# Fused windowed attention and token/channel mixer: scores of both halves in one row-tiled run, regroups moved to a second buffer pair, and emission order on all engines

## The chip, the cores and the metric

One NeuronCore of a Trainium2 chip. The metric is the device time of one execution in microseconds (us), median over several runs. Ratios are the mean time of one kernel's fast runs over the mean of the other's fast runs of the same rounds, so they are not quite the ratio of the medians quoted.

The time of one and the same kernel moves by up to 1% with the start of the program. Secondly, what comes after that point repeats well: wherever two kernels have the same items in a stage, the stage's length agreed within some 0.02 us. So beside the whole time I use **the stretch**: from the first weight load of tok1 of batch 1 to the last weight load of the program. It is read from the trace.

## The reference, cut to what matters

```python
# q, k, v: (8 batches, 8 heads, 576 positions, 64)
scores = scale * q @ k.T;  mask: 0 <= q_pos - k_pos < 128, with a slope per head
x = softmax(scores) @ v                       # per head, then heads side by side: (8, 576, 512)
h = relu(x.T @ w_tok1) @ w_tok2               # token mixing, 576 -> 256 -> 576
u = x + h.T
out = u + relu(u @ w_ch1) @ w_ch2             # channel mixing, 512 -> 1536 -> 512
```

## The kernel before

All matmuls and transposes run on TensorE (PE), with VectorE (DVE) and ScalarE (ACT) copying their results out of PSUM, the memory that they are written to. A "regroup" is a VectorE copy that puts a batch's q or k in the order that the transposes read. Attention goes by pairs of heads, g = 4 * batch + pair. The attention of batch b+1 is "side" work, spread between the mixer's items of batch b by weights. A pair needs four steps: transposes of q and k (`att_T`), scores with exp and mask in two halves (`att_S`), the product with the values (`att_V`). The scores are "row-tiled": each matmul uses 64 of TensorE's 128 rows, one head on each half. "Emission order" is the order in which the program names the instructions.

```python
ps_at = tile_pool(bufs=2, PSUM)     # two slots of two banks: transposes, scores, values
ps_ma = tile_pool(bufs=4, PSUM)     # four slots of one bank: the mixer

def regroup(b, h0, h1, which=(0, 1)):            # VectorE, one buffer qg, one kg
    for n in which:
        raw, t = ((qn, qg), (kn, kg))[n]
        nc.vector.tensor_copy(out=t[...], in_=raw[b % 2][...].rearrange("p h (j d) -> p j h d", j=6))

def att_T(g):
    ...                                          # 12 transposes of qg, kg into one two-bank tile
    nc.scalar.copy(out=dst(qT[g % 4]), in_=nat(0))
    nc.vector.tensor_copy(out=dst(kT[g % 4]), in_=nat(1))
    if hp == 3 and 0 < b < B - 1:
        regroup(b + 1, 0, H)                     # behind the last pair of a batch
        if b + 3 < B: dma_qk(b + 3, 0, H)

def att_S(g, half):
    sp = ps_at.tile([P, 2, 512], f32)            # a slot
    ...                                          # 4 or 6 matmuls with 64 of 128 rows, heads on
                                                 # rows 0-63 and 64-127
    for i in range(2): nc.scalar.activation(out=pe[:, i, :], in_=sp[:, i, :], func=Exp, ...)
    nc.vector.tensor_tensor(out=pb, in0=pe, in1=masks[...], op=mult)

def att_V(g):
    ...                                          # 18 matmuls into ot, then on VectorE:
    nc.vector.reciprocal(out=rt, ...);  nc.vector.tensor_tensor(out=xb[b][...], in0=ot, in1=rt)

def att_step(g):
    return [(0.6, att_T(g + 2)), (0.5, att_S(g + 1, 0)), (0.5, att_S(g + 1, 1)), (0.6, att_V(g))]

# mixer of a batch: tok1, tok2 (ht; VectorE: ub = ht + xb), trans_u (ut; VectorE: UT = ut),
# ch1 (ct; ScalarE: relu -> R), and ch2 of the batch before (o2; VectorE: obt = o2 + ub)

with tc.manual_schedule():                       # start, batch 0, attention of batch 1
    ...
with tc.manual_schedule(engines={PE}):           # the rest: PE in emission order, the other
    ...                                          # engines as a scheduler orders them
```

The softmax here doesn't subtract the row's maximum and nothing guards it: scores larger than these inputs give would overflow.

## Time and profile before

| | before |
|---|---|
| median | 334.01 us (333.99 to 334.29) |
| span of the profiled run | 332.9 us |
| the stretch (tok1 of batch 1 to the end) | 263.68 us |

The page of the kernel before: busy time by engine, and the clock in tenths over 40 slices of the span.

```profile
PE 307.6 (92%) x2816; PEld 189.1 (57%) x2816; DVE 178.9 (54%) x340; ACT 178.5 (54%) x373; POOL 60.9 (18%) x81
...
PEclk9999989999799999999999999999999999999999
```

PE is the bound. But "busy" hides what matters here, as matmuls overlap and their ends are modelled: one has to look at the distance from one start to the next. Within a stage these distances are constant (121.5 ns for 288 columns, 216 ns for 512). Whatever is above them is a loss, and losses are small here. The next lines are the timeline of PE alone: start, time, operation, count.

```profile
172.49 0.39 PE L234 MATMUL sp<-qT_93,kT_97 64*128 64x256 bf16 x4
172.81 1.64 PE L352 MATMUL ct<-UT,WC_105 128*128 128x288 bf16 x12
174.39 0.39 PE L234 MATMUL sp<-qT_93,kT_97 64*128 64x256 bf16 x6
174.71 0.54 PE L352 MATMUL ct<-UT,WC_105 128*128 128x288 bf16 x3
```

The two runs of `sp` (scores) are the two halves of one pair. The last ct ahead of the first run starts at 172.266 us. Its stream takes 120 ns, yet the first score starts 219 ns after it: 99 ns are lost. The stream of the last two scores takes 107 ns and the next ct comes 202 ns after them: some 95 ns more. With the second run the same again. One run of scores costs 0.19 us beside its streams, and this happens 48 times in the stretch.

The waits view for PE from 60 us on (total, times, longest):

```profile
PE ct L352 <- DVE UT L346: 2.7, 1, 2.7
PE t_957 L311 <- DVE xb L276: 1.2, 1, 1.2
PE ht L324 <- DVE ub L328: 1.1, 3, 0.4
```

The first of them, in the timeline of all engines:

```profile
81.19 0.74 DVE L212 COPY kT_100<-tT 128x576 bf16<-128x576 bf16 x1
...
81.86 0.95 DVE L143 COPY qg<-qn_86 96x3072 bf16<-96x3072 bf16 x1
82.72 0.95 DVE L143 COPY kg<-kn_88 96x3072 bf16<-96x3072 bf16 x1
...
83.59 1.54 DVE L346 COPY UT<-ut 128x576 bf16<-128x576 bf16 x4
...
84.09 1.49 PE L352 MATMUL ct<-UT,WC_105 128*128 128x288 bf16 x4 [2.67 <-DVE UT L346]
```

VectorE copies kT, then regroups q and k, and only then copies UT, for which PE has waited since 81.4 us. The windows view (length, busy us of PE, PEld, DVE, ACT, POOL, then the granted clock, DMA) shows what follows:

```profile
84.00:88.00 4.00, 3.74 (x16) 1.43 (x15) 1.67 (x5) 1.98 (x4) 0.81 (x2) 0.61 0.89 115
```

The clock is at 0.61 on the mean of these 4 us: in the trace it is at half from 84.9 to 88.3 us, for 3.4 us.

### The profile page before, as it was taken

Reading aid. Unit: us, or ns where it says so; the run is one execution under the profiler, and the core shown is the slowest. Engines: PE = TensorE matmul, PEld = TensorE weight load, DVE = VectorE, ACT = ScalarE, POOL = GpSimd, SP = SyncE. Lnnn points to the kernel's source line nnn. Section 1 sums busy time; section 2 is a strip of 40 time slices with the busy share of each in tenths; the row PEclk is TensorE's granted clock in tenths of the full one; section 3 lists DMA queues with packets and bytes.
Section 4 is the critical chain, followed back from the end, with each engine's and each line's share of the span. In section 5 each row is a group of like instructions: output and inputs, shape, how many; then the busy total and the mean of one; then the engine's idle time right before and its main releaser. Section 6 shows DMA issues by size and latency. Waiting matters only on the chain.

```text
span 332.9 us, 6713 instructions
## 1 busy us (share of the span) xinstructions
PE 307.6 (92%) x2816; PEld 189.1 (57%) x2816; DVE 178.9 (54%) x340; ACT 178.5 (54%) x373; POOL 60.9 (18%) x81
## 2 busy tenths in 40 slices
PE   2568799897899999999999999999999999999995
PEld 1244467554576456744676456744775457646742
DVE  5775834749544685339633785339633763244021
ACT  3861589063595436953495436953594338413800
POOL 8983153130105010041005000040000000000000
PEclk9999989999799999999999999999999999999999
DMA  7999999994908691094807510090100210011022
GB/s 92 137 157 205 207 164 156 213 187 62 140 4 52 83 175 66 1 103 82 158 2 50 86 63 33 2 103 33 64 2 7 58 65 32 2 63 65 0 65 96
DMA packets 59502, 27.76 MB, mean 83 GB/s; under 512 B 38672, under 2 KB 54864, under 8 KB 59472
## 3 DMA queue, kind: packets, MB, share of 16 engines
q0 software_dynamic: 54224, 17.90, 55.2%
q1 hardware_dynamic: 5248, 9.44, 8.6%
q8 instruction: 22, 0.36, 0.5%
q14 instruction: 8, 0.07, 0.1%
HBM read 35.78 MB, written 9.44 MB: 136 GB/s over the span
## 4 chain that ended last, share of the span: by engine, by line
PE 82%; DVE 11%; issue 2%; ACT 2%; DMA 2%; POOL 1%; POOLq 0%
PE ct L352 30%; PE sp L234 5%; PE ot L268 5%; PE tT L202 4%; PE ht L324 3%; DVE ub L328 2%; PE ut L341 2%; DVE kg L143 2%; DMA kn_87<-in_k_dram 2%; DVE pb L246 1%; ACT pe L242 1%; DVE qg L143 1%; DVE kT_100 L212 1%; DVE xb L276 1%; PE o_3667 L380 1%
## 5 line engine op out<-in xcount | busy, mean ns | idle before, releaser
L352 PE MATMUL ct<-UT,WC_105 128*128 128x288 bf16 x768 | 106.0, 290 | 2.8 <-DVE UT L346 2.7
L242 ACT ACTIVATE pe<-sp,biascol 128x512 bf16<-128x512 f32 x128 | 81.0, 692 | 28.6 <-PE sp L234 28.4
L357 ACT ACTIVATE R_102<-ct 128x288 bf16<-128x288 f32 x192 | 72.7, 422 | 30.4 <-PE ct L352 24.7
L352 PEld LDWEIGHTS <-WC_105 128*128 128x128 bf16 x768 | 72.1, 99 | 26.1 <-issue 6.7
L246 DVE TENSOR_TENSOR pb<-pe,masks 128x1024 bf16<-128x1024 bf16 x64 | 44.1, 689 | 65.0 <-ACT pe L242 64.8
L380 PEld LDWEIGHTS <-R_102 128*128 128x128 bf16 x432 | 39.3, 98 | 41.4 <-issue 1.1
L128 POOL DMA_DIRECT2D vp_92<-in_v_dram x16 | 14.8, 936 | 70.5 <-PE ot L268 64.7
L268 PEld LDWEIGHTS <-pb 128*128 128x128 bf16 x576 | 23.1, 102 | 6.9 <-DVE xb L276 2.5
L276 DVE TENSOR_TENSOR xb<-ot,rt 128x640 bf16<-128x640 f32 x32 | 26.3, 823 | 1.0
L328 DVE TENSOR_TENSOR ub<-ht,xb 128x512 bf16<-128x512 f32 x40 | 25.9, 680 | 1.3 <-PE ht L324 1.1
L324 PE MATMUL ht<-r1t,W_104 128*128 128x512 bf16 x80 | 22.1, 380 | 1.2 <-DVE ub L328 1.1
L202 PEld LDWEIGHTS <-qg 96*128 96x128 bf16 x192 | 12.4, 105 | 14.8 <-DVE qg L143 10.1
L128 POOL DMA_DIRECT2D vp_91<-in_v_dram x12 | 10.6, 890 | 46.5 <-PE ot L268 39.6
L311 PEld LDWEIGHTS <-W_103 128*128 128x128 bf16 x80 | 7.9, 104 | 12.5 <-issue 5.6
L211 ACT COPY qT_96<-tT 128x576 bf16<-128x576 bf16 x7 | 4.5, 639 | 19.5 <-PE tT L202 19.4
L268 PE MATMUL ot<-vp_91,pb 128*128 128x65 bf16 x288 | 13.2, 206 | 1.8 <-DVE xb L276 1.7
L346 DVE COPY UT<-ut 128x576 bf16<-128x576 bf16 x32 | 13.2, 450 | 1.1 <-PE ut L341 1.0
L212 DVE COPY kT_99<-tT 128x576 bf16<-128x576 bf16 x7 | 5.3, 757 | 14.2 <-ACT qT_95 L211 14.2
L211 ACT COPY qT_93<-tT 128x576 bf16<-128x576 bf16 x7 | 4.5, 639 | 15.8 <-PE tT L202 15.7
L324 PEld LDWEIGHTS <-W_104 128*128 128x128 bf16 x80 | 7.0, 98 | 9.8 <-issue 3.1
L202 PE MATMUL tT<-ident,qg 96*128 96x96 bf16 x168 | 12.2, 210 | 0.0
L202 PE MATMUL tT<-ident,kg 96*128 96x96 bf16 x168 | 12.0, 209 | 0.0
(186 smaller groups left out, 363.8 us busy)
## 6 DMA issues: line engine op xcount, KB each, us to landing
out_dram<-obt SPq DMA_DIRECT2D x32, 256.0 KB, 2.0
qn_86<-in_q_dram POOLq DMA_DIRECT2D x4, 576.0 KB, 7.5
kn_88<-in_k_dram POOLq DMA_DIRECT2D x4, 576.0 KB, 10.2
vp_92<-in_v_dram POOLq DMA_DIRECT2D x16, 128.0 KB, 7.3
qn_85<-in_q_dram POOLq DMA_DIRECT2D x3, 576.0 KB, 13.5
kn_87<-in_k_dram POOLq DMA_DIRECT2D x3, 576.0 KB, 16.4
WC_105<-in_moe_w_ch_dram POOLq DMA_DIRECT2D x3, 512.0 KB, 15.1
WC_106<-in_moe_w_ch_dram POOLq DMA_DIRECT2D x1, 1536.0 KB, 23.4
```

The costliest lines, as they stand in the source:

```text
L128: nc.gpsimd.dma_start(out=vp[b % 2][:, c, :, 0:D], in_=v[b, :, c * P : (c + 1) * P, :].rearrange("h s d -> s h d"),)
L202: nc.tensor.transpose(tt[n][:, j * RP : (j + 1) * RP], t_raw[:RP, j, 2 * hp : 2 * hp + 2, :].rearrange("p h d -> p (h d)"), ident[:RP, :RP],)
L234: nc.tensor.matmul(sp[:, hh, i * 256 + x0 : i * 256 + x1], lhsT=kt[r, k0 : k0 + P], rhs=qt[r, q0 : q0 + x1 - x0], start=True, stop=True,)
L242: nc.scalar.activation(out=pe[:, i, :], in_=sp[:, i, :], func=ACT.Exp, bias=biascol[:, h : h + 1], scale=scale,)
L246: nc.vector.tensor_tensor(out=pb[:, :, :], in0=pe[:, :, :], in1=masks[:, half, 2 * hp : 2 * hp + 2, :], op=ALU.mult,)
L268: nc.tensor.matmul(ot[:, i, qb * (D + 1) : (qb + 1) * (D + 1)], lhsT=pb[:, i, col : col + P], rhs=vb[:, kc, h, :], start=(n == 0), stop=(n ...
L276: nc.vector.tensor_tensor(out=xb[b][:, :, 2 * hp * D : (2 * hp + 2) * D].rearrange("p c (i d) -> p i c d", i=2), in0=o4[:, :, :, 0:D], in1 ...
L324: nc.tensor.matmul(ht[:, :], lhsT=W2[:, j, c0(c) : c0(c) + P], rhs=r1s[b, j][:, :], start=(j == 0), stop=(j == NDH - 1),)
L328: nc.vector.tensor_tensor(out=ubs[b][:, c, :], in0=ht[:, :], in1=xb[b][:, c, :], op=ALU.add)
L352: nc.tensor.matmul(ct[:, :], lhsT=WC1[:, cb, ht_i * P : (ht_i + 1) * P], rhs=UT[:, cb, o : o + SH], start=(cb == 0), stop=(cb == NCB - 1),)
L357: nc.scalar.activation(out=R2[:, ht_i, o : o + SH], in_=ct[:, :], func=ACT.Relu)
L380: nc.tensor.matmul(o2[0][:, :], lhsT=R2[:, ht_i, col : col + P], rhs=WC2[:, ht_i, :], start=(ht_i == 0 and c != NF), stop=(ht_i == NHT - 1),)
```

## The change

Its intent: (M) fewer entries into and exits from row-tiled work, by running both halves of a pair's scores together; (R) regroups out of the busy tok2 stage into ch1, with q and k buffers of their own for odd and even batches; (O) all engines in emission order. The diff is abridged.

```diff
-pbpool bufs=9, opool bufs=4
+pbpool bufs=8, opool bufs=3
-qg = const.tile(...)              ; kg the same
+qg = [const.tile(...) for i in range(2)] ; kg the same     # used as qg[b % 2]
@@ att_T
-        if hp == NHP - 1 and 0 < b < B - 1:
-            regroup(b + 1, 0, H)
-            if b + 3 < B: dma_qk(b + 3, 0, H)
@@ scores: att_S(g, halves) is the matmuls alone, att_E(g, half) two exps, att_M(g, half) the mask
+    def score_items(g):
+        return [
+            (0.5, lambda: (att_S(g, (0, 1)), att_E(g, 0))),
+            (0.4, lambda: (att_E(g, 1), att_M(g, 0))),
+            (0.3, lambda: att_M(g, 1)),
+        ]
@@ mixer_items, ch1
+                if ht_i in (4, 7) and 0 < b < B - 3:
+                    its.append((0.0, lambda n=ht_i // 7: regroup(b + 3, 0, H, (n,))))
+                if ht_i == 7 and 0 < b < B - 5:
+                    its.append((0.0, lambda: dma_qk(b + 5, 0, H)))
@@ after the values of batch 1 (66 us)
-    with tc.manual_schedule(engines={ENG.PE}):
+        regroup(2, 0, H)
+        if B > 4: dma_qk(4, 0, H)
+        side = [att_T(8), att_T(9)] + score_items(8) + att_step(8)
+        side.append((0.3, lambda: regroup(3, 0, H, (0,))))
+        side.append((0.3, lambda: regroup(3, 0, H, (1,))))
+        side.append((0.0, lambda: dma_qk(5, 0, H)))
+        side += att_step(9), (10), (11)
```

More of the change, by code (lines that the diff above doesn't have):

```diff
@@ L78 @@
     pepool = ctx.enter_context(tc.tile_pool(name="pe", bufs=3))
-    pbpool = ctx.enter_context(tc.tile_pool(name="pb", bufs=9))
+    pbpool = ctx.enter_context(tc.tile_pool(name="pb", bufs=8))
     xpool = ctx.enter_context(tc.tile_pool(name="xp", bufs=2))
@@ L83 @@
     upool = ctx.enter_context(tc.tile_pool(name="up", bufs=2))
-    opool = ctx.enter_context(tc.tile_pool(name="op", bufs=4))
+    opool = ctx.enter_context(tc.tile_pool(name="op", bufs=3))
     ps_at = ctx.enter_context(tc.tile_pool(name="ps_at", bufs=2, space=bass.MemoryType.PSUM))
@@ L90 @@
     kn = [const.tile([P, H, TPP * D], bf16, name=f"kn{i}") for i in range(2)]
-    qg = const.tile([P, TPP, H, D], bf16, name="qg")
-    kg = const.tile([P, TPP, H, D], bf16, name="kg")
+    qg = [const.tile([P, TPP, H, D], bf16, name=f"qg{i}") for i in range(2)]
+    kg = [const.tile([P, TPP, H, D], bf16, name=f"kg{i}") for i in range(2)]
     vp = [const.tile([P, NCH, H, D + 1], bf16, name=f"vp{i}") for i in range(2)]
@@ L143, in regroup @@
             nc.vector.tensor_copy(
-                out=t[:RP, :, h0:h1, :],
+                out=t[b % 2][:RP, :, h0:h1, :],
                 in_=raw[b % 2][:RP, h0:h1, :].rearrange("p h (j d) -> p j h d", j=TPP),
@@ L191 @@
     pbs = {}
+    sps = {}
+    pes = {}
     def att_T(g, early=False):
@@ L203, in att_T @@
                     tt[n][:, j * RP : (j + 1) * RP],
-                    t_raw[:RP, j, 2 * hp : 2 * hp + 2, :].rearrange("p h d -> p (h d)"),
+                    t_raw[b % 2][:RP, j, 2 * hp : 2 * hp + 2, :].rearrange("p h d -> p (h d)"),
                     ident[:RP, :RP],
@@ L212, in att_T, with att_S, att_E @@
         (nc.scalar.copy if early else nc.vector.tensor_copy)(out=dst(kT[g % NR]), in_=nat(1))
-        if hp == NHP - 1 and 0 < b < B - 1:
-            regroup(b + 1, 0, H)
-            if b + 3 < B:
-                dma_qk(b + 3, 0, H)
-    def att_S(g, half):
+    def att_S(g, halves):
         b, hp = divmod(g, NHP)
         qt, kt = qT[g % NR], kT[g % NR]
-        sp = ps_at.tile([P, 2, 512], f32, name="sp", tag="at")
-        for i in range(2):
-            kb = 2 * half + i
-            lastp = kb == NF - 1
-            w = P + TAIL if lastp else 2 * P
-            mms = [(0, w, kb * P, kb * P)]
-            if lastp:
-                mms.append((w, 2 * P, W0, NF * P))
-            for x0, x1, k0, q0 in mms:
-                for hh in range(2):
-                    r = slice(hh * D, (hh + 1) * D)
-                    nc.tensor.matmul(
-                        sp[:, hh, i * 256 + x0 : i * 256 + x1],
-                        lhsT=kt[r, k0 : k0 + P], rhs=qt[r, q0 : q0 + x1 - x0],
-                        start=True, stop=True,
-                    )
-        pe = pepool.tile([P, 2, 512], bf16, name="pe", tag="pe")
+        for half in halves:
+            sp = sps[g, half] = ps_at.tile([P, 2, 512], f32, name="sp", tag="at")
+            for i in range(2):
+                kb = 2 * half + i
+                lastp = kb == NF - 1
+                w = P + TAIL if lastp else 2 * P
+                mms = [(0, w, kb * P, kb * P)]
+                if lastp:
+                    mms.append((w, 2 * P, W0, NF * P))
+                for x0, x1, k0, q0 in mms:
+                    for hh in range(2):
+                        r = slice(hh * D, (hh + 1) * D)
+                        nc.tensor.matmul(
+                            sp[:, hh, i * 256 + x0 : i * 256 + x1],
+                            lhsT=kt[r, k0 : k0 + P], rhs=qt[r, q0 : q0 + x1 - x0],
+                            start=True, stop=True,
+                        )
+    def att_E(g, half):
+        b, hp = divmod(g, NHP)
+        sp = sps.pop((g, half))
+        pe = pes[g, half] = pepool.tile([P, 2, 512], bf16, name="pe", tag="pe")
         for i in range(2):
@@ L242, in att_S, with att_M, att_SEM @@
             nc.scalar.activation(
-                out=pe[:, i, :], in_=sp[:, i, :], func=ACT.Exp, bias=biascol[:, h : h + 1], scale=scale,
-            )
-        pb = pbpool.tile([P, 2, 512], bf16, name="pb", tag="pb")
+                out=pe[:, i, :], in_=sp[:, i, :], func=ACT.Exp,
+                bias=biascol[:, h : h + 1], scale=scale,
+            )
+    def att_M(g, half):
+        b, hp = divmod(g, NHP)
+        pb = pbs[g, half] = pbpool.tile([P, 2, 512], bf16, name="pb", tag="pb")
         nc.vector.tensor_tensor(
-            out=pb[:, :, :], in0=pe[:, :, :],
+            out=pb[:, :, :], in0=pes.pop((g, half))[:, :, :],
             in1=masks[:, half, 2 * hp : 2 * hp + 2, :], op=ALU.mult,
         )
-        pbs[g, half] = pb
+    def att_SEM(g, half):
+        att_S(g, (half,))
+        att_E(g, half)
+        att_M(g, half)
     def att_V(g):
@@ L289 @@
     NG = B * NHP
-    def att_step(g, g0=0, g1=NG, outputs=True):
+    def score_items(g):
[5 more added lines that the diff above has]
+    def att_step(g):
         its = []
-        if g0 <= g + 2 < g1:
+        if g + 2 < NG:
             its.append((0.6, lambda: att_T(g + 2)))
-        if g0 <= g + 1 < g1:
-            its.append((0.5, lambda: att_S(g + 1, 0)))
-            its.append((0.5, lambda: att_S(g + 1, 1)))
-        if g0 <= g < g1 and outputs:
+        if g + 1 < NG:
+            its += score_items(g + 1)
+        if g < NG:
             its.append((0.6, lambda: att_V(g)))
@@ L481 @@
         regroup(0, 2, 4)
-        att_S(0, 0)
+        att_SEM(0, 0)
         att_T(1, True)
         build_masks(1)
-        att_S(0, 1)
+        att_SEM(0, 1)
         regroup(0, 4, 6)
-        att_S(1, 0)
+        att_SEM(1, 0)
         att_T(2, True)
         build_masks(2)
-        att_S(1, 1)
+        att_SEM(1, 1)
         regroup(0, 6, 8)
@@ L493 @@
             dma_qk(2, 0, H)
-        att_S(2, 0)
+        att_SEM(2, 0)
         att_T(3, True)
         build_masks(3)
-        att_S(2, 1)
+        att_SEM(2, 1)
         att_V(0)
-        att_S(3, 0)
+        att_SEM(3, 0)
         att_V(1)
-        att_S(3, 1)
+        att_SEM(3, 1)
         att_V(2)
@@ L517 @@
             lambda: regroup(1, 0, H), lambda: att_T(g), lambda: att_T(g + 1),
-            t2[0], t2[1], lambda: att_S(g, 0), t2[2], t2[3], lambda: att_S(g, 1), t2[4],
-            lambda: att_S(g + 1, 0), *ut, lambda: att_S(g + 1, 1),
+            t2[0], t2[1], lambda: att_SEM(g, 0), t2[2], t2[3], lambda: att_SEM(g, 1), t2[4],
+            lambda: att_SEM(g + 1, 0), *ut, lambda: att_SEM(g + 1, 1),
         ]
@@ L525 @@
         side = [(0.6, lambda: att_T(g + 2))]
-        side += [(0.5, lambda x=x: att_S(g + 2, x)) for x in range(2)]
+        side += score_items(g + 2)
         side += [(0.6, lambda: att_T(g + 3))]
-        side += [(0.5, lambda x=x: att_S(g + 3, x)) for x in range(2)]
+        side += score_items(g + 3)
         spread([(0.48, f) for f in c1], side)
         spread(its1[:n1], [(0.6, lambda x=x: att_V(g + x)) for x in range(NHP)])
-    with tc.manual_schedule(engines={ENG.PE}):
-        side = att_step(2 * NHP - 2, 2 * NHP) + att_step(2 * NHP - 1, 2 * NHP)
-        for g in range(2 * NHP, 3 * NHP):
+        regroup(2, 0, H)
+        if B > 4:
+            dma_qk(4, 0, H)
+        side = [(0.6, lambda: att_T(2 * NHP)), (0.6, lambda: att_T(2 * NHP + 1))]
+        side += score_items(2 * NHP)
+        side += att_step(2 * NHP)
+        side.append((0.3, lambda: regroup(3, 0, H, (0,))))
+        side.append((0.3, lambda: regroup(3, 0, H, (1,))))
+        if B > 5:
+            side.append((0.0, lambda: dma_qk(5, 0, H)))
+        for g in range(2 * NHP + 1, 3 * NHP):
             side += att_step(g)
```

## The prediction

> **What bounds the kernel.** TensorE: the page gives PE 92% busy, DVE and ACT 54%; the chain of waits is 82% PE. From 61 us on (start-to-start distances of matmuls in the timeline), streaming is about 246.6 us and everything else 25 us:
> - about 9.5 us at 48 runs of scores, which use 64 of 128 rows. The first score starts about 97 ns later than the matmul ahead of it would allow, and the matmul after a run about 94 ns late. The Trainium skill, "TensorEngine Tiling (Array Packing)", Key Properties, says that changing the tiling mode drains the engine; this trace agrees, with 0.19 us per run.
> - 2.8 us in one wait near 81.2 us (waits view: ct on UT 2.7 us): VectorE does kT and the regroup of q and k (0.95 us each) before the UT copies. The clock then stands at half for 3.4 us (windows view), some 2.1 us more. "TensorE: Matmul & The Clock Gate", Part 1, describes such half-rate windows after idling.
> - about 1.9 us of waits inside tok2 (ht on ub), where the regroup stands among the ub additions.
> - 1.4 us ahead of tok1 at 65 us and 3.9 us at the end, both untouched, as are the first 40 us (some 20 us of idle PE).
>
> **What the change does.**
> 1. Both halves of a pair's scores run as one. 26 pairs (g = 6 to 31) lose one entry and one exit: 26 x 0.19 = 5.0 us, all on PE and so on the critical path. No matmul is added or removed.
> 2. Regroups leave the tok2/transpose stretch (VectorE 8.8 to 9.9 of 10 us busy) for ch1 (3 to 4 of 10), on a second pair of qg/kg buffers. That removes the 81 us stall with its half clock, about 4.8 us, and most tok2 waits, about 1.5 us.
> 3. VectorE and ScalarE now follow emission order. In before's ch1 ScalarE stood nearly so (2 exps, 3 relus, 2 exps), so this alone brings little.
>
> **What it costs.** The two score tiles take both slots of the two-slot PSUM pool, so the second half waits for the copies of the transposes two items earlier. In ch1 12 ct matmuls (1.45 us) stand between, against 1.2 to 1.4 us for the copies, more when ScalarE (9 of 10 us busy) is behind or a regroup precedes kT. Regroup of batch 2 moves to just after the last xb, at 66 us, so the transposes of pairs 8 and 9 wait some 0.5 us. In-order VectorE may wait for an exp ahead of ub or xb. I put 1.7 us on all of this.
>
> **Sum.** 334.0 - 5.0 - 4.8 - 1.5 + 1.7 = 324.4 us. Range 321.0 to 329.5. Chances: faster by over 2% 0.82, within 2% 0.16, slower 0.02.
>
> **What would show it.** (1) Score runs of 10 matmuls, one per pair, still 0.19 us each; (2) no ct-on-UT wait near 81 us, full clock in all windows after 45 us, regroup in ch1; (3) ht-on-ub waits near nothing; (4) new PE waits (scores on qT or kT copies, transposes on qg near 66 us) under 2 us in total; (5) end and first 40 us unchanged.
>
> **What would make it wrong.** Waits of scores on qT/kT copies in every ch1 stretch (up to 0.5 us x 14); ScalarE so far behind that ct waits for relu; the load of q, k for batch 4, issued only after the regroup at 66 us, not landed when ch1's regroup wants it near 88 us, which would stop in-order VectorE and idle PE into another half-clock stretch.

## The result and the profile after

The change took 332.77 us in the median (331.88 to 332.91, 4 runs) against 334.01 us, ratio 0.9955 (95% interval 0.9937 to 0.9974): 0.45% faster, where 2.9% was forecast. The stretch went from 263.68 to 262.09 us, 1.6 us less, where about 10 us less had been expected.

The page after:

```profile
PE 300.5 (91%) x2786; PEld 193.0 (58%) x2816; DVE 179.1 (54%) x340; ACT 177.3 (54%) x373; POOL 60.8 (18%) x81
...
PEclk9999989999999999999999999999999999999999
```

PE busy fell by 7 us, the span by 2. Some of that fall is no gain but missing records: 2786 matmuls were recorded instead of 2816, while weight loads are complete (2816), so I measured distances by the weight loads.

The timeline of PE after, where one merged run stands:

```profile
169.26 1.64 PE L370 MATMUL ct<-UT,WC_107 128*128 128x288 bf16 x12
170.83 0.61 PE L233 MATMUL sp<-qT_95,kT_99 64*128 64x256 bf16 x10
171.38 1.40 PE L370 MATMUL ct<-UT,WC_107 128*128 128x288 bf16 x10
```

Ten scores in one run, entered 99 ns late and left as before. Split, the two halves took 850 ns from the end of the stream before to the start of the matmul after (99 + 123 + 202 and 99 + 205 + 122); merged it is 645 ns (99 + 424 + 122). So 205 ns a pair are saved, as predicted. The waits of PE after, from 60 us on:

```profile
PE ut L355 <- DVE UT L364: 2.0, 2, 1.0
PE ct L370 <- DVE UT L364: 1.6, 2, 0.9
...
PE ut L355 <- DVE ub L346: 1.2, 1, 1.2
PE tT L204 <- DVE kg_91 L143: 0.6, 1, 0.6
PE ct L370 <- ACT R_104 L375: 0.6, 4, 0.2
PE sp L233 <- DVE kT_100 L214: 0.5, 2, 0.3
```

The waits of ht on ub are gone, and the one of 2.7 us as well, but there are several new kinds. The last two lines are waits at matmuls that a busy PE half hides; in start distances they are larger (below). First the stretch around batch 1's u-transposes, all engines:

```profile
80.06 0.82 DVE L287 TENSOR_TENSOR xb<-ot,rt 128x640 bf16<-128x640 f32 x1
80.80 0.68 DVE L346 TENSOR_TENSOR ub<-ht,xb 128x512 bf16<-128x512 f32 x1
...
81.54 0.23 PE L355 MATMUL ut<-swap,ub 128*128 128x128 bf16 x1 [1.20 <-DVE ub L346]
...
81.99 0.95 DVE L143 COPY qg_90<-qn_86 96x3072 bf16<-96x3072 bf16 x1
...
82.86 0.95 DVE L143 COPY kg_92<-kn_88 96x3072 bf16<-96x3072 bf16 x1
...
83.73 0.81 DVE L364 COPY UT<-ut 128x576 bf16<-128x576 bf16 x2
...
84.23 0.65 PE L370 MATMUL ct<-UT,WC_107 128*128 128x288 bf16 x2 [0.89 <-DVE UT L364]
...
85.62 0.65 PE L370 MATMUL ct<-UT,WC_107 128*128 128x288 bf16 x2 [0.75 <-DVE UT L364]
```

The regroup of batch 3 (L143) did not go to ch1. It stands in the same place as before, between the first u-transposes and the UT copies. Ahead of it, the reciprocal and xb of `att_V` stand before the last ub, so the u-transposes wait too. The clock, however, held this time:

```profile
84.00:88.00 4.00, 2.86 (x25) 1.70 (x25) 2.00 (x6) 1.70 (x4) 0.95 (x2) 1.00 0.86 112
```

The second new place, batch 3 (and the same in batch 5), first after, then before:

```profile
157.50 0.21 DVE L286 RECIPROCAL rt<-ot 128x10 f32<-128x10 f32 x1
...
157.61 0.39 PE L359 MATMUL ut<-ident,ub 128*128 128x128 bf16 x4
157.75 0.82 DVE L287 TENSOR_TENSOR xb<-ot,rt 128x640 bf16<-128x640 f32 x1
...
158.49 1.54 DVE L364 COPY UT<-ut 128x576 bf16<-128x576 bf16 x4
158.99 0.22 PE L355 MATMUL ut<-swap,ub 128*128 128x128 bf16 x1 [0.99 <-DVE UT L364]
```

```profile
159.45 0.21 DVE L275 RECIPROCAL rt<-ot 128x10 f32<-128x10 f32 x1
...
159.60 0.46 DVE L346 COPY UT<-ut 128x576 bf16<-128x576 bf16 x1
...
159.97 0.81 DVE L276 TENSOR_TENSOR xb<-ot,rt 128x640 bf16<-128x640 f32 x1
...
160.70 1.17 DVE L346 COPY UT<-ut 128x576 bf16<-128x576 bf16 x3
```

Emission order puts both parts of `att_V`'s evacuation (0.21 and 0.82 us) ahead of all UT copies. The u-transposes fill the mixer's PSUM slots, and the fourth group waits 0.99 us for a copy to free one. Before, the scheduler had slipped one UT copy between the reciprocal and xb (159.60 us), and there was hardly a wait.

Summed up over the stretch (distances between weight loads, beyond the constant distance of the stage; us):

| loss on PE | before | after |
|---|---|---|
| entering and leaving score runs, 48 and 24 runs | 9.3 | 4.6 |
| wait of ct at 81 us, two short waits of ct on UT after it (84.1, 84.5 us), half-clock matmuls | 2.84 + 0.5 + 1.7 | 0 |
| ht on ub in tok2 | 1.8 | 0 |
| around batch 1's u-transposes: ut on ub, ct on UT twice | in the line above | 3.8 |
| transposes of pair 8 on the regroup at 67 us | 0 | 0.8 |
| second half of merged scores on a kT copy (70.9, 75.5, 92.4, 99.0 us) | 0 | 1.4 |
| u-transposes in batches 3 and 5 | 0.3 | 2.3 |
| ct on relu in ch1, batches 2 to 6 | 0 | 2.1 |

The new waits, the last five lines, come to 10.4 us. The prediction had 1.7 us for them.

### The profile page after: what moved, and what is told of

Its sections match the earlier page's. It is cut to its first block, busy times and chain, and to the rows that moved or that the text cites. A ratio compares the mean times of both kernels' runs of the same rounds, so it can differ in the third digit from the quotient of the medians.

```text
span 330.9 us, 6654 instructions
## 1 busy us (share of the span) xinstructions
PE 300.5 (91%) x2786; PEld 193.0 (58%) x2816; DVE 179.1 (54%) x340; ACT 177.3 (54%) x373; POOL 60.8 (18%) x81
## 4 chain that ended last, share of the span: by engine, by line
PE 75%; DVE 12%; ACT 8%; issue 2%; DMA 2%; POOL 1%; POOLq 0%
PE ct L370 24%; PE ot L279 5%; ACT pe L245 4%; PE sp L233 4%; PE tT L204 4%; PE ht L342 4%; DVE ub L346 2%; DVE pb L253 2%; DMA qn_85<-in_q_dram 2%; PE ut L359 1%; DVE xb L287 1%; DVE obt L410 1%; DVE kT_100 L214 1%; ACT R_104 L375 1%; PE o_4136 L398 1%
## 5 line engine op out<-in xcount | busy, mean ns | idle before, releaser
L370 PE MATMUL ct<-UT,WC_107 128*128 128x288 bf16 x768 | 103.9, 287 | 2.4 <-DVE UT L364 1.6
L245 ACT ACTIVATE pe<-sp,biascol 128x512 bf16<-128x512 f32 x128 | 80.0, 690 | 23.2 <-PE sp L233 16.8
L370 PEld LDWEIGHTS <-WC_107 128*128 128x128 bf16 x768 | 72.8, 98 | 24.3 <-issue 4.9
L398 PEld LDWEIGHTS <-R_104 128*128 128x128 bf16 x432 | 40.4, 98 | 43.1
L342 PE MATMUL ht<-r1t,W_106 128*128 128x512 bf16 x75 | 20.5, 379 | 0.4 <-issue 0.3
L279 PE MATMUL ot<-vp_93,pb 128*128 128x65 bf16 x288 | 13.2, 206 | 1.9 <-DVE xb L287 1.7
L329 PEld LDWEIGHTS <-W_105 128*128 128x128 bf16 x80 | 7.8, 103 | 12.0 <-issue 4.8
L286 DVE RECIPROCAL rt<-ot 128x10 f32<-128x10 f32 x32 | 6.9, 216 | 13.2 <-PE ot L279 13.1
L204 PEld LDWEIGHTS <-qg_89 96*128 96x128 bf16 x96 | 6.1, 106 | 11.7 <-DVE qg_89 L143 9.9
L279 PE MATMUL ot<-vp_94,pb 128*128 128x65 bf16 x288 | 11.4, 193 | 0.1
L359 PE MATMUL ut<-ident,ub 128*128 128x128 bf16 x128 | 11.1, 226 | 0.0
```

The source lines that it names most:

```text
L204: nc.tensor.transpose(tt[n][:, j * RP : (j + 1) * RP], t_raw[b % 2][:RP, j, 2 * hp : 2 * hp + 2, :].rearrange("p h d -> p (h d)"), ident[: ...
L279: nc.tensor.matmul(ot[:, i, qb * (D + 1) : (qb + 1) * (D + 1)], lhsT=pb[:, i, col : col + P], rhs=vb[:, kc, h, :], start=(n == 0), stop=(n ...
L342: nc.tensor.matmul(ht[:, :], lhsT=W2[:, j, c0(c) : c0(c) + P], rhs=r1s[b, j][:, :], start=(j == 0), stop=(j == NDH - 1),)
L359: nc.tensor.transpose(ut[:, main0 + c * P : main0 + (c + 1) * P], ubs[b][:, c, cb * P : (cb + 1) * P], ident[:, :],)
L370: nc.tensor.matmul(ct[:, :], lhsT=WC1[:, cb, ht_i * P : (ht_i + 1) * P], rhs=UT[:, cb, o : o + SH], start=(cb == 0), stop=(cb == NCB - 1),)
L398: nc.tensor.matmul(o2[0][:, :], lhsT=R2[:, ht_i, col : col + P], rhs=WC2[:, ht_i, :], start=(ht_i == 0 and c != NF), stop=(ht_i == NHT - 1),)
```

## The experiments

Each run was compared with the kernel before on the same chip. All outputs are right. M, R and O name the three parts of the change. Two theories went in. The *order theory*: merging pays, and what is lost is lost to VectorE's strict order and to where the regroups stand. The *slot theory*: two score tiles take both slots of the two-slot pool and bring four exps close together, so that merging makes its own waits.

| kernel | median us | ratio to before (95%) | stretch us |
|---|---|---|---|
| before | 333.1 to 334.0 | | 263.68 |
| the change (M, R, O) | 332.77 | 0.9955 (0.9937 to 0.9974) | 262.09 |
| M | 332.72 | 0.9962 (0.9920 to 1.0005) | 262.47 |
| M, R | 347.26 | 1.0401 (1.0347 to 1.0455) | 260.79 |
| M, O | 336.20 | 1.0054 (0.9979 to 1.0128) | 265.44 |
| O | 340.32 | 1.0198 (1.0153 to 1.0243) | 270.02 |
| R, O | 335.15 | 1.0051 (0.9987 to 1.0115) | 265.68 |
| change, regroups of batches 2, 3 moved | 329.24 | 0.9892 (0.9840 to 0.9944) | 259.09 |
| change, UT copies shared with ScalarE | 328.29 | 0.9869 (0.9821 to 0.9918) | 259.98 |
| change, four exps apart | 332.04 | 0.9961 (0.9907 to 1.0015) | 261.80 |
| change, wider exp gap | 332.00 | 0.9946 (0.9912 to 0.9980) | 261.63 |
| M, R, with the regroups moved | 329.45 | 0.9885 (0.9845 to 0.9925) | 258.98 |
| change, regroups moved, UT shared | 327.71 | 0.9812 (0.9778 to 0.9846) | 257.06 |
| change, all three mends | 327.48 | 0.9793 (0.9756 to 0.9830) | 256.95 |

### 1. Merging alone (M)

```diff
 # before, and
+att_S(g, (0, 1)), att_E, att_M and score_items(g) as in the change; nothing else
```

> Before, with the two halves of each pair's scores in one run (10 matmuls) and nothing else: regroups where they were, the scheduler still orders VectorE and ScalarE in the second part. Order theory (merging pays what its row-tiled runs save, 26 x 0.205 = 5.3 us, and the loss lies in VectorE's strict order and in where the regroups stand): 328.5 to 330, score runs of 424 ns without waits in the stretches after 105 us. Slot theory (two score tiles in a two-slot PSUM pool, and four exps close together, bring their own waits that eat the gain): 332.5 or more, with waits of scores on kT and of ct on relu also here.

The stretch fell by 1.2 us, not by 5. The loss at 82 us stayed, with a wait of 1.70 us and its half-clock window, and ct waited for relu four times 0.31 us. The score runs of batches 2 to 6 were clean in ch1 and tok1 (424 ns), but those in tok2 took 635 to 953 ns, and the early ones 813 to 1013 ns: the second half waited for a kT copy, 3.4 us in all. The time, and both kinds of wait, are what the slot theory had said: with both slots needed at once, a run stops in its middle when the transposes' copies are late. But the 1.5 us of this in tok2 is also a matter of place: VectorE's timeline has the scheduler put the regroup ahead of that kT copy (in batch 2 both copies, at 113.33 and 114.20 us, with kT at 115.07 us; in batch 3 one of them), and in experiment 3, where emission order puts kT first, the same runs took 424 ns. The Trainium skill, "TensorEngine Tiling (Array Packing)", PSUM Bottleneck, warns that copies out of PSUM may become the bottleneck once tiling has sped TensorE up; here TensorE gained by fewer entries and exits, not by more tiling, and the copies held it up for 0.2 to 0.6 us in a run.

### 2. Merge and regroup, scheduler order (M, R)

```diff
 # the change, but for the part after 66 us
+    with tc.manual_schedule(engines={ENG.PE}):
```

> The change without its third part: merged scores and moved, double-buffered regroups, but the scheduler orders VectorE and ScalarE in the second part. Order theory: the 1.15 us waits of the u-transposes in batches 3 and 5 and the 3.8 us around the u-transposes of batch 1 are gone or much smaller, so 323.5 to 327. Slot theory: 331 to 333, like the change as a whole.

Both theories missed: 347 us. One wait did it, in ch1 of batch 0, outside the stretch. The waits view and VectorE's part of the timeline:

```profile
PE sp L233 <- DVE kT L214: 18.0, 5, 16.9
```

```profile
48.11 0.69 DVE L253 TENSOR_TENSOR pb<-pe,masks 128x1024 bf16<-128x1024 bf16 x1 [1.40 <-ACT pe L245]
...
49.63 0.64 ACT L213 COPY qT<-tT 128x576 bf16<-128x576 bf16 x1
...
64.10 0.96 DVE L143 COPY qg<-qn 96x3072 bf16<-96x3072 bf16 x1 [15.30 <-DMA qn<-in_q_dram]
```

With a second pair of buffers nothing but its own load holds the regroup of batch 3 back, so the scheduler hoisted it ahead of the kT copy of pair 7. That load (issued at 50.56 us, landed at 63.98 us) stopped VectorE for 15.3 us, and everything behind it. The Trainium skill, "TensorE: Matmul & The Clock Gate", lists VectorE's and ScalarE's queues as strict first-in, first-out in the row "Engine queue depth" of its opening table; the trace agrees, since the qT copy of pair 7, on ScalarE, was ready at 50.3 us, and the kT copy that goes with it did not pass the regroup. This shows what O is for in the change: not speed, but keeping R's new freedom in check. In the stretch, which begins after this stop, the waits that the order theory had named did shrink: to 0.33 and 0.86 us in batches 3 and 5, and to 1.9 us around batch 1's u-transposes, where batch 3's regroup no longer stands.

### 3. Merge and order (M, O), and 4. order alone (O)

```diff
 # before (O), or experiment 1 (M, O); the part after 66 us
-    with tc.manual_schedule(engines={ENG.PE}):
+    # in the manual_schedule() of all engines
```

> Merged scores and emission order on all engines, regroups as before (single buffer, emitted behind the last transposes of a batch). Order theory: strict order with the regroup in the tok2 stretch is worst: 332 to 336, waits of u-transposes or tok2 of 1 us and more in most batches, and the 81 us stall stays. Slot theory: about as merging alone.

> Before, with emission order on all engines and nothing else: split scores, old regroups. Order theory: slower than before, 335.5 to 339, the u-transposes waiting some 1.1 us in batches 3 and 5 where xb stands ahead of the UT copies. Slot theory: 333.5 to 334.5, as the scheduler's order was nearly this one.

The order theory had the direction and the waits right, but both kernels came out above its ranges (336.20 us against 332 to 336, 340.32 us against 335.5 to 339). Order alone cost 6.3 us of the stretch: 2.5 us at 82.6 us, with half clock for 6.8 us after it (3.4 us before), up to 1.4 us in tok2 of batches 2 to 5 where the regroup of 1.8 us stood between ub additions, and about 1 us of u-transposes in batches 3 and 5. With the merge the stretch was 4.6 us shorter than with order alone. Some 1.7 us of that is the clock, which stood at half for 3.4 us here; the rest, 2.9 us, is what merging brought in strict order, out of 4.9.

### 5. Regroup and order without the merge (R, O)

```diff
 # the change, and
-        return [(0.5, S both halves + E0), (0.4, E1 + M0), (0.3, M1)]
+        return [(0.5, lambda x=x: att_SEM(g, x)) for x in range(2)]
```

> The change without its merged scores: split halves, moved regroups, emission order everywhere. If the merge pays its 26 x 0.205 us less the 1.4 us that its runs wait for kT: 335 to 338, some 4 us above the change, with the same u-transpose waits of about 1.1 us. If the merge brings most of the new waits itself (slot theory): at or below the change, 330 to 333.

335.15 us and a stretch of 265.68 us, against 262.09 with the merge: 3.6 us. Some 1.7 us of these are not the merge's own: this kernel's profile had a half-clock stretch of 3.4 us after 85 us, which the change's had not. (One of its four runs, of 332.08 us, had a mean clock of 1.000, so it cannot have had one; the other three took 335.04 to 335.83 us.) The merge's worth inside the change is then about 1.9 us. Its books agree roughly: 4.9 us saved, 1.4 us of waits within runs and 2.1 us of ct on relu given back, leaves 1.4 us. So the slot theory holds for a good part of the merge's gain. The u-transposes' waits of 1 us in batches 3 and 5 and the batch-1 losses stand here just as well, so they are not the merge's. In this kernel ct never waited for relu in batches 2 to 6; those waits come with the merge.

### 6. Regroups of batches 2 and 3 moved

```diff
-        spread(its1[:n1], [(0.6, att_V(g + x)) for x in range(4)])
-        regroup(2, 0, H);  dma_qk(4, 0, H)
+        side = [(0.6, att_V(g + x)) for x in range(4)]
+        side.insert(1, (0.0, lambda: regroup(2, 0, H, (0,))))
+        side.insert(3, (0.0, lambda: (regroup(2, 0, H, (1,)), dma_qk(4, 0, H))))
+        spread(its1[:n1], side)
+        regroup(3, 0, H);  dma_qk(5, 0, H)
@@ side of batch 1
-        side.append(... regroup(3) q), (... regroup(3) k), (... dma_qk(5))
```

> The changed kernel with only batch 2's and 3's regroups moved: batch 2's among the value products of batch 1 (VectorE about half busy there), batch 3's to where batch 2's stood (66 us), so nothing of them stands near the u-transposes of batch 1. Placement theory (3.8 us of waits around batch 1's u-transposes and ch1, 0.8 us of transposes on the regroup at 67 us and 0.6 us in two score runs come from where these two regroups stand): 3 to 5 us below the change, 328 to 330. Rival (in-order VectorE is short of time there anyway, since five ub, xb, two pb and an obt stand before the UT copies): under 1.5 us below, as the waits move by one item only.

The stretch lost 3.0 us. The waits on the regroup at 67 us (0.8 us) and around batch 1's u-transposes (3.8 us) shrank to 0.6 us plus 0.7 us of ct waits, while the runs of scores that wait for kT grew a little (1113 instead of 516 ns in one). Everything from batch 2 on stayed as it was, the two 1.15 us waits too.

### 7. Every second UT copy on ScalarE

```diff
-        nc.vector.tensor_copy(out=UT[:, cb, o : o + S], in_=ut[:, :])
+        copy = nc.scalar.copy if cb % 2 == 0 and b > 0 else nc.vector.tensor_copy
+        copy(out=UT[:, cb, o : o + S], in_=ut[:, :])
```

> The changed kernel with every second UT copy on ScalarE, which is idle some 5 us there. If the 1.15 us waits of batches 3 and 5 (and part of batch 1's) come from xb standing ahead of the UT copies in VectorE's strict order: 2 to 3.5 us below the change, 329.5 to 331, u-transposes without waits over 0.3 us. If they come from PSUM slots held by ch2's output instead: no gain, within 0.5 us of the change.

2.1 us off the stretch. (The whole time, 328.29 us, lies below the range expected. Its four runs had mean clocks of 0.995 to 1.000, the change's 0.993 to 0.994, so a part of that is the start and not the edit.) The same place in batch 3:

```profile
154.79 1.20 ACT L365 COPY UT<-ut 128x576 bf16<-128x576 bf16 x2 [2.18 <-PE ut L359]
154.81 0.21 DVE L286 RECIPROCAL rt<-ot 128x10 f32<-128x10 f32 x1
...
155.06 0.82 DVE L287 TENSOR_TENSOR xb<-ot,rt 128x640 bf16<-128x640 f32 x1
...
155.48 0.22 PE L355 MATMUL ut<-swap,ub 128*128 128x128 bf16 x1 [0.17 <-ACT UT L365]
```

ScalarE, idle until then, takes a copy while VectorE does the reciprocal and xb; the wait falls from 1.15 to 0.33 us. That the waits come from copies queued behind xb is shown by this. That a slot held by ch2's output has a share in the remaining 0.33 us was not tried.

### 8. Four exps one apart

```diff
-            (0.5, S both halves + E0), (0.4, E1 + M0), (0.3, M1)
+            (0.5, S both halves + exp 0 of half 0), (0.2, exp 1 of half 0),
+            (0.2, exp 0 of half 1, M0), (0.2, exp 1 of half 1), (0.2, M1)
```

> The changed kernel with its four exps of a pair as four separate items, one apart, instead of two and two. If the 0.16 to 0.32 us waits of ct in ch1 (about 2.2 us over batches 2 to 6) come from relus queued behind pairs of exps: those waits shrink below 0.1 us each, 1 to 2 us below the change, 331 to 332. If ScalarE is simply short of time in ch1: they stay or grow, 332.5 to 334.

The ct waits of ch1 vanished in batches 2 to 5 (1.9 us less), so relus behind pairs of exps were their cause. But only 0.3 us of it reached the stretch. The changed weights shifted the items, and three runs of scores now waited for kT (930, 930 and 1376 ns), two of them because they stood too close behind transposes (the third, now 1376 ns, had waited before: 814 ns). One of these:

```profile
179.00 1.03 PE L402 MATMUL o<-WC,R 128*128 128x512 bf16 x4
179.20 0.64 ACT L213 COPY qT<-tT 128x576 bf16<-128x576 bf16 x1 [2.05 <-PE tT L204]
179.88 0.76 DVE L214 COPY kT<-tT 128x576 bf16<-128x576 bf16 x1 [2.54 <-ACT qT L213]
179.96 0.22 PEld L233 LDWEIGHTS <-kT 64*128 64x128 bf16 x5 [0.42 <-issue]
...
180.69 0.40 PE L233 MATMUL sp<-qT,kT 64*128 64x256 bf16 x6 [0.33 <-DVE kT L214]
```

Only four matmuls (0.86 us) stand between transposes and scores. In the change a tok1 of 1.08 us stood there as well. The kT copy begins when the qT copy has ended, so both take 1.44 us, and the second half waits 0.33 us for the slot.

### 9. A wider gap between the pairs of exps

```diff
-            (0.4, lambda: (att_E(g, 1), att_M(g, 0))),
+            (0.6, lambda: (att_E(g, 1), att_M(g, 0))),
```

> The changed kernel with one number changed: the second half's exps and the first mask product weigh 0.6 in the spread instead of 0.4, so that three relus instead of two stand between the two pairs of exps in ch1. If the ct waits of 0.16 to 0.32 us in batches 2 to 6 are relus queued behind exps that stand too close, they vanish and nothing replaces them: about 1.9 us off the stretch from tok1 of batch 1 to the end (262.1 to some 260.2 us), 330 to 332 in all. If ScalarE is short of time there, the waits stay.

Half right: the four waits of 0.32 us in batches 2 and 4 went to 0.16 us, the others stayed, and two runs of scores in tok2 now waited for kT (500 and 497 ns); 0.5 us off the stretch.

### 10. Merge and regroup again, with batch 3's regroup pinned

```diff
 # experiment 2, with the regroups of batches 2 and 3 placed as in experiment 6
```

> Merged scores and moved regroups with the scheduler ordering VectorE and ScalarE (as the 347 us run), but batch 3's regroup pinned behind batch 2's, inside the part that keeps emission order. If the 16.9 us wait of that run came from the scheduler hoisting batch 3's regroup ahead of its load (the second buffers no longer forbid it), it is gone: 328 to 331, and from the first tok1 of batch 1 to the end 258 to 261 us against 259.1 us in the same kernel with emission order. If the scheduler itself is at fault with merged scores, a wait of over 5 us stands elsewhere.

The 16.9 us wait was gone and the kernel took 329.45 us. Its stretch (258.98 us) equals that of the same kernel in emission order (259.09 us). So strict order costs nothing on balance once these two regroups are well placed; it cost 6.3 us with the old regroups and 1.3 us with the change's, because of what stood where. (The 1.3 us is the change against M, R, where batch 3's regroup had run before the stretch, so the place of that regroup is part of it.)

### 11. Two mends, and 12. three mends together

```diff
 # experiments 6 and 7 together (11), and 9 on top (12)
```

> Both mends that worked alone (regroups of batches 2 and 3 moved: 3.0 us off that stretch; every second UT copy on ScalarE: 2.1 us off). If they mend different waits: 256.5 to 257.5 us from tok1 of batch 1 to the end, 325 to 328 in all. If both lived off the same waits around batch 1's u-transposes: 258 to 259 us.

> All three mends together: regroups of batches 2 and 3 moved, every second UT copy on ScalarE, wider gap between the exps. If the three losses are separate: 254.5 to 256 us from tok1 of batch 1 to the end, 322.5 to 326.5 in all, faster than before by over 2%. If a new wait takes their place: 257 us or more.

The two mends add up: 5.0 us off the change's stretch (3.0 + 2.1 alone). The third gave 0.1 us on top instead of 0.5: two runs in tok2 wait for kT (498 ns each) as they had in experiment 9, and one in ch1 (810 ns), which had not waited in experiment 11, does so now. The upper end of what I had expected, 256 us, was missed by 1 us. With a ratio of 0.9793 to the kernel before, the version with all three has the lowest, though its 95% interval (0.9756 to 0.9830) overlaps that of the two mends and does not exclude that the gain is just under 2%.

R without M and O, and M-R-O in which kT's copy does not wait for qT's, were not run.

## Why the prediction was wrong

The range (321.0 to 329.5 us) missed 332.77 us, and the error lies nearly all in one term.

1. *Merging saves 26 x 0.19 = 5.0 us.* Right: 205 ns for each of the 24 pairs in the stretch, 4.9 us (4.7 us in the table, which counts entries and exits alone), and two pairs before it. Runs of 10 at the same entry and exit cost are in the trace. That changing the tiling mode drains PE ("TensorEngine Tiling (Array Packing)", Key Properties) agrees with the 99 ns at each entry.
2. *"Regroups leave the tok2/transpose stretch for ch1"; 4.8 us and 1.5 us.* Right for batches 4 to 7: the tok2 waits, 1.8 us, are gone. Wrong for batch 3, the very one behind the 81 us stall: the diff appends it to the side list behind `att_V(8)`, and in VectorE's order it stands between obt and the UT copies. I had not looked up its place. The stall came back as 3.8 us in three pieces. The half-clock window, 1.7 us, was saved, perhaps by luck: with R and O without M, pieces of 1.9, 1.05 and 0.9 us brought it back in the profile, but not in every run (experiment 5). Moving this regroup and batch 2's (experiment 6) won 3.0 us.
3. *"VectorE and ScalarE now follow emission order … this alone brings little."* Wrong: alone it cost 6.3 us with the clock's share (experiment 4). I had compared the order of ScalarE in ch1 and not that of VectorE at the u-transposes, where before had one UT copy ahead of xb and after has none. In the change it costs 1.3 us net (experiments 10 and 6 show that this comes with the placement, above all that of batch 3's regroup, and not with order as such), and it spares a 16.9 us stop that the second buffers would allow (experiment 2).
4. *"I put 1.7 us on all of this."* This is the step that failed. The new waits measured 10.4 us: 3.8 us at batch 1's u-transposes, 2.3 us at those of batches 3 and 5, 2.1 us of ct on relu, 1.4 us of second halves on kT, 0.8 us of transposes on the regroup. Of these the prediction had named the last three kinds: kT and the regroup among its costs, relu only as a danger. It gave a size only for the regroup (0.5 us against 0.8) and, as a danger, an upper bound for kT (0.5 us x 14). It named neither the losses at batch 1's u-transposes nor the waits of batches 3 and 5, 6.1 us together, where VectorE's strict order puts `att_V`'s copies, and at batch 1 a regroup, ahead of what TensorE waits for (experiments 6 and 7).
5. *End and first 40 us unchanged; clock full after 45 us.* Right: 3.9 us at the end in both, and no slice after the start shows less than full clock. The load of batch 4's q and k also landed in time (78.3 and 81.9 us).

So: 4.9 us of merging, 5.0 us of stall and clock and 1.8 us of tok2 were saved, 11.7 us in all. New waits took back 10.4 us. With the 0.3 us that batches 3 and 5 had waited before, the stretch fell by 1.6 us.

## What to carry to other kernels

When a scheduler's order is replaced by emission order, list each engine's instructions at every place where TensorE waits for an evacuation, and count what now stands ahead of it; an engine that is 54% busy on the mean can still be the one that holds the next matmul. Savings found by measuring distances on the bound engine were right here to 0.3 us, while the costs, which depend on what stands next to what, were off by a factor of six: size each possible wait at its place, and take an unnamed one as likely. A second buffer removes a dependency that may have been the only thing keeping an instruction late, so pin such an instruction, or a load that is not there yet will stop a whole in-order engine.

## What the Trainium skill lacked or had wrong

- "TensorEngine Tiling (Array Packing)", Key Properties, says that a change of tiling mode drains the engine and gives no figure. Here: 99 ns at the entry to a row-tiled run of 64 rows and some 95 ns at its exit, the same with 4, 6 and 10 matmuls in the run.
- "TensorE: Matmul & The Clock Gate", Part 1, gives idling of about 3.4 us as what halves the clock (its practical rule, in "Why this matters for your kernels": no gaps over about 3 us). Here a gap of 2.67 us near 81.4 us was followed by half clock for 3.4 us (mean 0.61 over 84 to 88 us), and so was one of 1.70 us in experiment 1. Losses of 1.57, 1.05 and 0.9 us within 6 us (the changed kernel) were not, and 1.90, 1.05 and 0.9 us (experiment 5) were, in the profiled run but not in all of its four. What decides it beside the length of a gap, these runs do not show.
- No page that I read says that matmul records can be missing while the weight loads' are complete: 2786 against 2816 in the changed kernel's profile. Distances between weight loads were the better measure.
